# First Strassen group of an attention and gated-MLP kernel: GpSimd makes lower halves, conversions are dealt anew, x gets a third staging buffer

## The chip, the cores and the metric

The kernel runs on one core of a Trainium2 chip. The metric is the device time of one execution in microseconds (us), as the median of several runs. The engines are called by the names of the profile: PE (TensorE, matmuls; PEld are its weight loads), DVE (VectorE), ACT (ScalarE), POOL (GpSimd) and SP (SyncE, which here issues most of the DMAs). A DMA issued by an engine stands in that engine's queue, in order with its other instructions.

## The reference, cut to what matters

```python
# q, k, v: (8, 8, 576, 64)   w_gate, w_val: (512, 1536)   w_out: (1536, 512)
scores = q @ k.T / 8, masked by blocks of 64 (block_i >= block_j)
x = softmax(scores) @ v                 # put together to 4608 tokens x 512
gate = 1 / (1 + exp(-(x @ w_gate)))
out = (gate * (x @ w_val)) @ w_out      # 4608 x 512, float32
```

The three weights arrive as float64. The kernel turns them into float32 itself, by bit operations on the two words of each number. The products need more precision than one pass of PE in the type float32r gives, so every factor is split into an upper half H (rounded to float32r) and a lower half L (what is left), and each product is made as H·H + H·L + L·H, three matmuls.

## The kernel before, in words

**Stages.** Up to about 621 us the kernel does the attention, and between its matmuls the MLP for the first 512 of the 1536 hidden features. The attention's result x goes to DRAM (`xT_d`), the first part of the output too (`part_d`). The other 1024 hidden features are done in two Strassen groups `g` of 512 each. Each group goes over all tokens in five blocks `k`: four of 1024 tokens and one of 512. The list `passes` holds the ten (group, block) pairs; in the first group the order is 0, 1, 4, 2, 3 (block 4 is the small one, so it is the third), in the second 0, 1, 2, 3, 4. The first group writes its part of the output to `part2_d`, the second adds both parts to its own and writes `out`.

**A block.** `unit` (L931) is one of four pairs (q, gv): q is one half of the group's features, gv is gate or value. A unit makes seven Strassen products (`product`, six matmuls each) into three PSUM banks A, B and C out of six, and DVE adds them up (L952 to L965); ACT copies the first of them out (p, L937) and makes the tanh (L944). For gv = 1 DVE then multiplies gate and value (L948), and `split_h` (L926) splits the result h: ACT casts it into hH (L928), and the subtraction for hL (L929) is made by POOL for q = 0 and by DVE for q = 1. After the units, `out_block` (L993) makes the eight output tiles of the block (four in the small one), two groups of four one behind the other, each in two halves of the hidden features (first those of q = 0). In the first group ACT copies each tile out of PSUM (`ost`, L1018), and SP stores it (L1019). There are two tiles of two halves for that, four buffers in turn.

**x of the next block.** `x_load` (L774) brings a quarter of a block's x (half of the columns `c0` by half `j` of d_model) into a staging buffer `XB`, of which there are two. POOL makes the first of the sums that Strassen needs (L793), `x_split` (L798) the others on DVE (L806), the H on ACT (L808) and the L on DVE (L809). The H and L of all seven forms go to the tiles `XO`, over those of the block before. The two loads for the first half of the columns stand at the start of the block before, their split at its end; then come the two loads and the split for the second half.

**Conversions.** While the first group runs, the second group's weights are converted in 24 pieces (the list `later`): 16 of w_gate and w_val, then 8 of w_out. A piece is loaded by SP (`raws`, two buffers), made float32 by six DVE operations and an ACT square (`to_f32`, L676, lines L685 to L699), for w_gate and w_val combined to the seven forms by four more (L742 to L745), cast by ACT into the upper half of a tile `st` (L751, L771), and DVE subtracts for the lower half (L752, L772). SP stores `st` in DRAM (`wgv_d`, `wo_d`). The float32 tile `T` is there once, `st` twice. `do_later(k, i)` (L1109) says how many pieces go behind unit i of a block, or behind its output products (i = 4). In the last block of the first group each unit's weights `W` are refilled from `wgv_d` as soon as the unit is done (L1156), and `wo` at the end.

**Order.** A list scheduler, which works with modelled costs, puts each engine's instructions in order before the program runs; the program's order is its priority, and an instruction that is not ready by the model lets later ones go first. `behind(a, b)` only keeps a after b on one engine's list. On the chip each engine then works off its list in order.

Of the kernel before, what the change touches and what calls it, by code (L numbers as in the profile page):

```python
# [9 lines left out]
F32 = mybir.dt.float32  # L10
# [10 lines left out]
N2 = 512  # L21
# [23 lines left out]
def attn_glu_kernel(ctx: ExitStack, tc: tile.TileContext, q, k, v, w_gate, w_val, w_out, out):  # L45
# [126 lines left out]
    with ExitStack() as s2:  # L172
# [404 lines left out]
        def tiles_o(i):  # L577
            if not co_:
                co_.extend(cv.tile([P, 4, NX], U32, name="XB", bufs=2) for _ in range(2))
                co_.append(at.tile([P, 512], U32, name="coT"))  # L580
            co = [x.rearrange("p a n -> p (a n)") for x in co_[:2]]
            return (co[i % 2].rearrange("p (n w) -> p n w", w=2), co_[2], None,
                    mp.tile([P, 512], F32, name="csq", tag="ost", bufs=2))
# [134 lines left out]
        def half_tiles():  # L718

            i = n_cv[0] % 2  # L720
            n_cv[0] += 1
            if not halves:
                halves.append(cv.tile([P, 2, 256, 2], U32, name="raws", tag="rqk0"))
                halves.append(io.tile([P, 8, P // 2], F32, name="T"))
            return halves[0][:, i], halves[1]
# [21 lines left out]
        def split_gv(T, dst, alone=False):  # L747
            if alone:
                nc.vector.tensor_copy(out=dst[:, 0], in_=T[:, :7])
            else:  # L750
                nc.scalar.copy(out=dst[:, 0], in_=T[:, :7])  # L751
            return nc.vector.tensor_sub(out=dst[:, 1], in0=T[:, :7], in1=dst[:, 0].bitcast(F32)).ins  # L752
# [14 lines left out]
        def wo_piece(raw, T, dst, held=False):  # L767
# [4 lines left out]
            nc.vector.tensor_sub(out=dst[:, 1], in0=T[:, :m], in1=dst[:, 0].bitcast(F32))  # L772

        def x_load(k, j, c0):  # L774

            t0, nk = blocks[k]
            XB = cv.tile([P, 4, NX], F32, name="XB", bufs=2)
# [147 lines left out]

        def split_h(q, i, hH, hL, h, nk):  # L926
            f, n = ((q, 0), (q, nk), (q + 2, 0), (q + 2, nk))[i]
            nc.scalar.copy(out=hH[:, f, n:n + nk], in_=h)  # L928
            (nc.vector if q else nc.gpsimd).tensor_sub(out=hL[:, f, n:n + nk], in0=h, in1=hH[:, f, n:n + nk].bitcast(F32))  # L929
# [63 lines left out]
        def out_block(g, k, hH, hL, wo, sums, more, end):  # L993
            t0, nk = blocks[k]
            n = nk // P
            for ts in (range(n, 2 * n), range(n)):
# [15 lines left out]
                for t in ts:  # L1012
                    r = t0 + t * P
                    if g == 0:
                        if t % 2 == 0:
                            two = cv.tile([P, 2, DM], F32, name="ost2", tag="KQ", bufs=2)
                        ost = two[:, t % 2]
# [35 lines left out]
        io = pool("io")  # L1053
# [19 lines left out]
        for n, (q, gv) in enumerate(units):  # L1073
            for j in range(KC):
                for half in range(2):
# [3 lines left out]
                    def one(got, n=n, j=j, half=half):  # L1079
                        st = st_tile(7, P // 2)  # L1080
                        sums_gv(*got, True)
                        split_gv(got[1], st)
# [3 lines left out]
        for f in range(4):  # L1086
            for half in range(2):
# [3 lines left out]
                def one(got, f=f, half=half):  # L1091
                    st = st_tile(1, DM // 2)[:, :, 0]
                    wo_piece(*got, st, True)
# [3 lines left out]

        n_st = [0]

        def st_tile(a, n):  # L1100

            n_st[0] += 1
            if n_st[0] % 2:
                return cv.tile([P, 2, a, n], F32R, name="st", tag="rqk1")
            return io.tile([P, 2, a, n], F32R, name=f"st{a}", tag="st")
# [3 lines left out]
        def do_later(k, i):  # L1109

            if k == 0:
                count = 2 if i == 4 else 0
            else:
                count = 1 if i < 4 or blocks[k][1] < N2 else 2
# [6 lines left out]

        hH = hp2.tile([P, 4, 2 * N2], F32R, name="hH2")
        hL = hp2.tile([P, 4, 2 * N2], F32R, name="hL2")
        for i, (g, k) in enumerate(passes):
            nk = blocks[k][1]
            end = i == len(passes) - 1
            turn = i + 1 < len(passes) and passes[i + 1][0] > g
            rest_x = []
            if not end:
# [11 lines left out]
                if nn == nk:  # L1141
                    rest_x = [c0 for c0 in range(NX, nn, NX)]
# [5 lines left out]
            for n, (q, gv) in enumerate(units):  # L1148
# [3 lines left out]
                if g + 1 < G:  # L1152
                    do_later(k, n)
                    if turn:
                        W[q, gv] = wgv_tile(q, gv)
                        nc.sync.dma_start(out=W[q, gv].bitcast(F32), in_=wgv_d[n])  # L1156
            if not end:
                x_split(XBs, 0, last2["DVE"])
                for c0 in rest_x:
                    XBs = x_pair(kn, c0)  # L1160
                    for XB in XBs:
                        x_sums(XB, nc.gpsimd)
                    x_split(XBs, c0)
# [36 lines left out]
```

## Time and profile before

| | |
|---|---|
| time, median of 3 runs | 1171.35 us (1170.59 to 1173.22) |
| the profiled execution: its own time, its span | 1172.55 us, 1170.4 us |
| granted clock of TensorE, mean | 0.997 |
| PE busy | 1143.3 us (98%) |
| DVE busy | 813.4 us (69%) |
| ACT busy | 607.9 us (52%) |
| POOL busy | 306.5 us (26%) |
| DMA | 153.32 MB, mean 131 GB/s |

A row of a group or of a timeline names the line of the kernel, the engine, the operation and out<-in by the program's names for tiles, with buffer numbers left out. "[1.21 <-DVE v L952]" behind a row of a timeline means that the engine stood idle for 1.21 us before it and that the DVE instruction of line 952 that writes v ended the wait. The table by stretches gives for each engine the busy us and, in parentheses, the number of instructions; with the name of a tile it counts only the instructions that write or read this tile. Matmuls overlap at their ends, so the step from start to start tells their pace, not their duration.

### The profile page before, as it was taken

The numbers are of one execution on the slowest core, as the hardware profiler recorded it, in microseconds if no ns is written. First come the engines' busy times: TensorE is split into PE (matmuls) and PEld (weight loads), VectorE is DVE, ScalarE is ACT, GpSimd is POOL, SyncE is SP. The second block draws the span as 40 slices with busy tenths as digits, with TensorE's granted clock in tenths as the row PEclk, the third lists the DMA queues.
The fourth block names the chain that finished last, engine by engine and source line by source line (L and its number), as shares of the span: only waits on it lengthen the run. The fifth ranks groups of instructions, "written<-read, shape, count | busy, mean of one in ns | idle before, by whom it ended". The sixth has DMA issues, their size and how long they took to land.

```text
span 1170.4 us, 18756 instructions
## 1 busy us (share of the span) xinstructions
PE 1143.3 (98%) x6413; PEld 916.2 (78%) x6413; DVE 813.4 (69%) x1533; ACT 607.9 (52%) x1344; POOL 306.5 (26%) x356
## 2 busy tenths in 40 slices
PE   6799999999999999999999999999999999999998
PEld 4466777877877787787888888988877888888887
DVE  5678754554655555466989879899897675758565
ACT  5677765756766766675344444544544323233222
POOL 4345513222322313233002110211111424141402
PEclk9999999999999999999999999999999999999999
DMA  8675443444355354525243152763769452635342
GB/s 198 167 153 119 101 118 83 112 98 114 81 116 114 72 124 102 119 69 152 83 134 108 43 169 66 211 163 75 211 261 297 144 198 90 191 97 175 113 135 64
DMA packets 300431, 153.32 MB, mean 131 GB/s; under 512 B 227248, under 2 KB 267184, under 8 KB 299696
## 3 DMA queue, kind: packets, MB, share of 16 engines
q1 hardware_dynamic: 288960, 132.42, 42.9%
q10 hardware_dynamic: 10992, 18.65, 4.4%
q8 instruction: 51, 0.84, 0.3%
q0 software_dynamic: 384, 1.05, 0.2%
q14 instruction: 44, 0.36, 0.1%
HBM read 104.73 MB, written 47.33 MB: 130 GB/s over the span
## 4 chain that ended last, share of the span: by engine, by line
PE 80%; DVE 9%; DMA 4%; issue 3%; ACT 2%; SPq 1%; POOL 1%; ACTq 0%; DVEq 0%; POOLq 0%
PE b L919 25%; PE bank L266 13%; PE m L139 13%; PE m L146 7%; PE b L1004 7%; PE m L1004 7%; PE bank L270 6%; PE bank L139 2%; DVE XL L809 1%; DMA XB<-xT_d 1%; PE m L270 1%; PE bank L146 1%; DMA raws<-in_moe_w_out_dram 1%; ACT G L371 1%; DMA rqk<-in_q_dram 1%
## 5 line engine op out<-in xcount | busy, mean ns | idle before, releaser
L919 PE MATMUL b<-XH,w 128*128 128x512 f32 (+1 forms) x1120 | 320.8, 368 | 3.0 <-ACT XH L808 1.7
L919 PEld LDWEIGHTS b<-XH,w 128*128 128x128 f32 x1120 | 203.4, 189 | 39.3 <-ACT XH L808 2.2
L919 PE MATMUL b<-XL,w 128*128 128x512 f32 (+1 forms) x560 | 205.6, 368 | 0.1
L399 ACT ACTIVATE P<-bank,nm 128x512 f32<-128x512 f32 (+3 forms) x256 | 132.4, 539 | 35.6 <-DVE nm L391 34.6
L919 PEld LDWEIGHTS b<-XL,w 128*128 128x128 f32 x560 | 105.6, 189 | 18.1 <-DVE XL L809 0.6
L808 ACT CAST XH<-XB 128x1024 fp32r<-128x1024 f32 (+1 forms) x72 | 66.9, 943 | 87.4 <-DVE XB L806 46.2
L391 DVE TENSOR_REDUCE nm<-bank 128x2 f32<-128x1024 f32 (+3 forms) x128 | 102.4, 821 | 3.0
L520 DVE TENSOR_TENSOR xT<-bank,rb 128x320 f32<-128x320 f32 x64 | 26.3, 452 | 110.3 <-PE bank L266 91.5
L371 ACT COPY G<-bank 128x768 f32<-128x768 f32 (+3 forms) x140 | 91.0, 700 | 13.1 <-PE bank L270 11.8
L793 POOL TENSOR_TENSOR XB<-XB 128x256 f32<-128x256 f32 x30 | 25.5, 850 | 273.8 <-DMA XB<-xT_d 211.2
L266 PE MATMUL bank<-G,VS 128*64 128x320 f32 (+4 forms) x896 | 94.1, 360 | 0.2
L1004 PE MATMUL m<-wo,hH 128*128 128x512 f32 x288 | 93.2, 389 | 0.0
L1004 PE MATMUL b<-wo,hH 128*128 128x512 f32 x288 | 92.6, 389 | 0.0
L809 DVE TENSOR_TENSOR XL<-XB,XH 128x1024 fp32r<-128x1024 f32 (+1 forms) x72 | 78.0, 1085 | 15.4 <-ACT XH L808 15.4
L266 PEld LDWEIGHTS bank<-G,VS 128*64 128x64 f32 x896 | 55.8, 137 | 41.3 <-issue 4.7
L146 PE MATMUL m<-wo,hH 128*128 128x512 f32 x256 | 86.9, 401 | 0.5 <-ACT hH L163 0.5
L139 PE MATMUL m<-XH,wv 128*128 128x512 f32 x240 | 83.6, 403 | 0.0
L139 PE MATMUL m<-XH,wg 128*128 128x512 f32 x240 | 82.9, 400 | 0.0
L533 POOL TENSOR_TENSOR XL<-xT,XH 128x512 fp32r<-128x512 f32 (+1 forms) x32 | 43.2, 1349 | 144.8 <-ACT XH L528 144.8
L270 PE MATMUL bank<-ident,P 128*128 128x128 f32 x560 | 71.2, 273 | 0.0
L270 PEld LDWEIGHTS bank<-ident,P 128*128 128x128 f32 x560 | 64.3, 140 | 8.3 <-issue 0.7
L164 POOL TENSOR_TENSOR hL<-h,hH 128x512 fp32r<-128x512 f32 x28 | 36.8, 1315 | 111.1 <-ACT hH L163 110.9
(195 smaller groups left out, 2349.3 us busy)
## 6 DMA issues: line engine op xcount, KB each, us to landing
XB<-xT_d SPq DMA_DIRECT2D x48, 256.0 KB
prr<-part_d SPq DMA_DIRECT2D x46, 256.0 KB
xT_d<-xT ACTq DMA_DIRECT2D x32, 288.0 KB
part_d<-ost SPq DMA_DIRECT2D x36, 256.0 KB
VS<-in_v_dram SPq DMA_DIRECT2D x64, 128.0 KB
part_d<-ost ACTq DMA_DIRECT2D x32, 256.0 KB
rqk<-in_k_dram SPq DMA_DIRECT2D x108, 72.0 KB
rqk<-in_q_dram SPq DMA_DIRECT2D x108, 72.0 KB
```

Source lines behind the costliest of these rows:

```text
L139: mm = nc.tensor.matmul(ps, lhsT=lh, rhs=rh, start=(i == 0), stop=(i == n - 1))
L146: mm = nc.tensor.matmul(ps, lhsT=lh[:, f, t * P:(t + 1) * P], rhs=rh, start=(f == i == 0), stop=(f == F1 - 1 and i == 2))
L266: pe_last[:] = [nc.tensor.matmul(*args, **kw).ins]
L270: pe_last[:] = [nc.tensor.transpose(*args).ins]
L371: mark("ACT", nc.scalar.copy(out=dst, in_=src))
L391: mark("DVE", nc.vector.tensor_reduce(out=nm[:, c0:c0 + 2], in_=ps[:, :, c:c + P * (i + 1)], axis=AX.X, op=ALU.max, negate=True))
L399: mark("ACT", nc.scalar.activation(out=Pi[:, h], in_=ps[:, h, c:c + n], func=AF.Exp, bias=nm[:, c0 + h:c0 + h + 1], accum_out=sm[:, 5 * h ...
L533: nc.gpsimd.tensor_sub(out=XL[:, hp, :w], in0=xT[:, :w], in1=XH[:, hp, :w].bitcast(F32))
L808: nc.scalar.copy(out=XO[j][0][:, a:b, c], in_=x)
L809: sub = nc.vector.tensor_sub(out=XO[j][1][:, a:b, c], in0=x, in1=XO[j][0][:, a:b, c].bitcast(F32))
L919: mm = nc.tensor.matmul(ps, lhsT=lh, rhs=rh, start=(first and k == 0), stop=(k == n - 1), skip_group_check=not first)
L1004: mm = nc.tensor.matmul(po[t], lhsT=lh[:, f, t * P:(t + 1) * P], rhs=rh, start=(half == 0 and i == 0), stop=(half == 1 and i == 5))
```

## The change

- `split_h`: in the first group POOL makes all of hL, for q = 1 too. In the second group DVE makes it for q = 1, as before.
- `split_gv` and `wo_piece`: for the 24 pieces POOL subtracts for the lower half, in place of DVE.
- `do_later`: the pieces are dealt otherwise. The five blocks of the first group, in their order, took 2, 6, 5, 6 and 5 pieces; now they take 2, 8, 4, 8 and 2, and the last two stand behind the first unit.
- Buffers: `T` is now there twice and `st` once; both lie in buffers of the pool `cv` that were there before, and the pool `io` is gone. For `ost` one tile of two halves is left, two buffers in turn.
- x: a third staging buffer `XB2` in a new pool `x3`; the three are used in turn. Of the second half of the columns, the load and the first sum for j = 0 now stand at the start of the block before; the load for j = 1 stands behind the split of the first half.
- `refill`: the refill of the last unit's weights now stands behind the loads and the split of x.

```diff
         def x_load(k, j, c0):
...
-            XB = cv.tile([P, 4, NX], F32, name="XB", bufs=2)
+            i = n_x[0] % len(stages)
+            n_x[0] += 1
+            XB = stages[i].tile([P, 4, NX], F32, name=f"XB{i}")
...
             if not halves:
                 halves.append(cv.tile([P, 2, 256, 2], U32, name="raws", tag="rqk0"))
-                halves.append(io.tile([P, 8, P // 2], F32, name="T"))
-            return halves[0][:, i], halves[1]
+                halves.append(cv.tile([P, 2, 7, P // 2], F32R, name="st", tag="rqk1"))
+                two, one = (cv.tile([P, 2, DM], F32, name=x, tag="KQ", bufs=2) for x in ("ost2", "T"))
+                halves.append([one[:, j].rearrange("p (s n) -> p s n", n=P // 2) for j in range(2)])
+                halves.append(itertools.cycle((two[:, 0], two[:, 1])))
+            return halves[0][:, i], halves[2][i]
...
-        def split_gv(T, dst, alone=False):
+        def split_gv(T, dst, alone=False, lower=nc.vector):
...
-            return nc.vector.tensor_sub(out=dst[:, 1], in0=T[:, :7], in1=dst[:, 0].bitcast(F32)).ins
+            return lower.tensor_sub(out=dst[:, 1], in0=T[:, :7], in1=dst[:, 0].bitcast(F32)).ins
...
-            (nc.vector if q else nc.gpsimd).tensor_sub(out=hL[:, f, n:n + nk], in0=h, in1=hH[:, f, n:n + nk].bitcast(F32))
+            (nc.vector if q and second[0] else nc.gpsimd).tensor_sub(out=hL[:, f, n:n + nk], in0=h, in1=hH[:, f, n:n + nk].bitcast(F32))
...
-                        if t % 2 == 0:
-                            two = cv.tile([P, 2, DM], F32, name="ost2", tag="KQ", bufs=2)
-                        ost = two[:, t % 2]
+                        if not halves:
+                            half_tiles()
+                        ost = next(halves[3])
...
-        io = pool("io")
+        stages.append(pool("x3"))
...
-                        st = st_tile(7, P // 2)
+                        st = halves[1]
                         sums_gv(*got, True)
-                        split_gv(got[1], st)
+                        split_gv(got[1], st, lower=nc.gpsimd)
...
-            if k == 0:
-                count = 2 if i == 4 else 0
+            place = turns_of[0].index(k)
+            if place in (0, NK - 1):
+                count = 2 if i == (0 if place else 4) else 0
             else:
-                count = 1 if i < 4 or blocks[k][1] < N2 else 2
+                count = (1, 1, 0, 1, 1)[i] if blocks[k][1] < N2 else (1, 2, 1, 2, 2)[i]
...
+        def refill(n):
+            W[units[n]] = wgv_tile(*units[n])
+            d = nc.sync.dma_start(out=W[units[n]].bitcast(F32), in_=wgv_d[n])
+            if n == len(units) - 1:
+                behind(d.ins, last2["SP"])
...
                 if nn == nk:
-                    rest_x = [c0 for c0 in range(NX, nn, NX)]
+                    rest_x = [x_load(kn, 0, NX)]
+                    x_sums(rest_x[0], nc.gpsimd)
...
-                    if turn:
-                        W[q, gv] = wgv_tile(q, gv)
-                        nc.sync.dma_start(out=W[q, gv].bitcast(F32), in_=wgv_d[n])
+                    if turn and n + 1 < len(units):
+                        refill(n)
             if not end:
                 x_split(XBs, 0, last2["DVE"])
-                for c0 in rest_x:
-                    XBs = x_pair(kn, c0)
-                    for XB in XBs:
-                        x_sums(XB, nc.gpsimd)
-                    x_split(XBs, c0)
+                if rest_x:
+                    rest_x.append(x_load(kn, 1, NX))
+                    x_sums(rest_x[1], nc.gpsimd)
+                    x_split(rest_x, NX)
+            if turn:
+                refill(len(units) - 1)
             run(outs)
```

More of the change, by code (lines that the diff above doesn't have):

```diff
@@ L578, in tiles_o @@
             if not co_:
-                co_.extend(cv.tile([P, 4, NX], U32, name="XB", bufs=2) for _ in range(2))
+                co_.extend(cv.tile([P, 4, NX], U32, name=f"XB{i}") for i in range(2))
                 co_.append(at.tile([P, 512], U32, name="coT"))
@@ L765, in fetch_wo, with wo_piece @@
             return raw, T
-        def wo_piece(raw, T, dst, held=False):
+        def wo_piece(raw, T, dst, held=False, lower=nc.vector):
             T = T.rearrange("p s n -> p (s n)")
@@ L771, in wo_piece @@
             nc.scalar.copy(out=dst[:, 0], in_=T[:, :m])
-            nc.vector.tensor_sub(out=dst[:, 1], in0=T[:, :m], in1=dst[:, 0].bitcast(F32))
+            lower.tensor_sub(out=dst[:, 1], in0=T[:, :m], in1=dst[:, 0].bitcast(F32))
+        stages, n_x = [cv, cv], [0]
         def x_load(k, j, c0):
             t0, nk = blocks[k]
-            XB = cv.tile([P, 4, NX], F32, name="XB", bufs=2)
+            i = n_x[0] % len(stages)
+            n_x[0] += 1
+            XB = stages[i].tile([P, 4, NX], F32, name=f"XB{i}")
             v = XB[:, 0:4].rearrange("p (kh th) n -> p kh th n", kh=2)
@@ L924, in product @@
             mark2("PE", mm)
+        second = [False]
         def split_h(q, i, hH, hL, h, nk):
@@ L1091, in one @@
                 def one(got, f=f, half=half):
-                    st = st_tile(1, DM // 2)[:, :, 0]
-                    wo_piece(*got, st, True)
+                    st = halves[1].rearrange("p e a n -> p e (a n)")[:, :, :DM // 2]
+                    wo_piece(*got, st, True, nc.gpsimd)
                     h = slice(half * DM // 2, (half + 1) * DM // 2)
@@ L1096, in attn_glu_kernel @@
                 later.append((get, one))
[L1098 to L1105, printed above, removed]
         got = []
         def do_later(k, i):
-            if k == 0:
-                count = 2 if i == 4 else 0
+            place = turns_of[0].index(k)
+            if place in (0, NK - 1):
+                count = 2 if i == (0 if place else 4) else 0
             else:
-                count = 1 if i < 4 or blocks[k][1] < N2 else 2
+                count = (1, 1, 0, 1, 1)[i] if blocks[k][1] < N2 else (1, 2, 1, 2, 2)[i]
             for _ in range(min(count, len(later))):
@@ L1125, in attn_glu_kernel @@
             nk = blocks[k][1]
+            second[0] = g > 0
             end = i == len(passes) - 1
```

## The prediction

> **What bounds the kernel now.** I read the page first, then the table of busy time by stretch of time, then PE's own timeline, and last the chain of waits at the place where PE loses time.
>
> ```profile
> span 1170.4 us, 18756 instructions
> ...
> PE 1143.3 (98%) x6413; PEld 916.2 (78%) x6413; DVE 813.4 (69%) x1533; ACT 607.9 (52%) x1344; POOL 306.5 (26%) x356
> ```
>
> PE is busy for 1143.3 of 1170.4 us, so no change that leaves the matmuls alone can win more than the 27 us in which PE stands still, and only what lies in the stage that is edited. The next view cuts out that stage: the five blocks of the first Strassen group (the fifth stretch ends where PE starts the second group), and one block of the second group below.
>
> ```profile
> core 0: us, PE busy (x) PEld busy (x) DVE busy (x) ACT busy (x) POOL busy (x), PEclk, DMA share, GB/s
> 621.00:681.00 60.00, 60.00 (x266) 49.66 (x265) 53.16 (x92) 29.47 (x46) 11.07 (x14) 1.00 0.30 96
> 681.00:741.00 60.00, 60.00 (x268) 49.72 (x267) 51.13 (x106) 28.16 (x48) 8.73 (x8) 1.00 0.48 131
> 741.00:777.00 36.00, 35.91 (x236) 32.84 (x235) 34.96 (x93) 17.93 (x40) 5.81 (x7) 1.00 0.59 160
> 777.00:837.00 60.00, 60.00 (x266) 49.64 (x266) 54.70 (x120) 28.98 (x49) 8.13 (x7) 1.00 0.55 143
> 837.00:894.00 57.00, 55.79 (x247) 45.88 (x246) 52.68 (x102) 25.30 (x46) 9.24 (x8) 1.00 0.75 263
> ...
> 955.80:1015.70 59.90, 59.90 (x266) 49.60 (x265) 40.40 (x59) 19.45 (x29) 20.35 (x16) 1.00 0.45 140
> ```
>
> The clock is granted in full (1.00) throughout. PE is full in four of the five blocks, and in the second group (59.90 of 59.90), where the change therefore has nothing to win. The second fullest engine is DVE, with 51 to 55 of 60 us, while POOL has 6 to 11. PE loses time in the fifth stretch alone and just behind it, so I looked there instruction by instruction. The first number of a row is its start.
>
> ```profile
> 865.93 0.39 PE L919 MATMUL b<-XH,w 128*128 128x512 f32 x1
> 867.53 0.50 PE L919 MATMUL b<-XH,w 128*128 128x512 f32 x1 [1.21 <-DVE v L952]
> ...
> 893.50 0.39 PE L919 MATMUL b<-XH,w 128*128 128x512 f32 x1
> 893.73 0.39 PE L919 MATMUL b<-XL,w 128*128 128x512 f32 x1
> 893.96 0.61 PE L919 MATMUL b<-XH,w 128*128 128x512 f32 x2
> 894.71 0.50 PE L919 MATMUL b<-XL,w 128*128 128x512 f32 x1
> 895.05 0.40 PE L919 MATMUL b<-XH,w 128*128 128x512 f32 x1
> 897.19 0.73 PE L919 MATMUL b<-XH,w 128*128 128x512 f32 x2 [1.74 <-ACT XH L808]
> ```
>
> Matmuls start 0.23 us apart when nothing holds them (893.50 to 893.73). From 865.93 to 867.53 are 1.60 us for one step: 1.37 lost, to a DVE add (L952) that was late behind conversion work. From 893.50 to 897.19 are six steps in 3.69 us: 2.33 lost, to the first x of the second group, not yet split. Together 3.70 us, the change's whole visible prize. The chain of waits tells why x was late (start, length):
>
> ```profile
> 861.42 9.37 DMA raws<-in_moe_w_out_dram
> ...
> 885.59 5.03 DMA XB<-xT_d
> 890.78 1.54 POOL XB L793
> ```
>
> and SP's queue tells when the load could go:
>
> ```profile
> 883.51 2.55 SPq L785 DMA_DIRECT2D XB<-xT_d  x4
> ```
>
> A piece of w_out took 9.37 us to land between the refills of w, DVE stood in order behind it, and both loads of the second half of x were issued only at 883.51, when the first half had been split and had freed both staging buffers. PE wanted them at 893.50.
>
> **The change, part by part.** *Third staging buffer, load moved ahead.* One of the two loads of the second half (two DMAs of the four, with the sums by POOL) now goes at the start of the block, 50 us earlier; the other still waits for a freed buffer. The last refill of w is put behind that load on SP, and of its four it is the one needed last. SP issues the same DMAs, so nothing is added there. On POOL's queue the early sum now stands ahead of the block's hL; the load needs some 5 us, and an hL of the second block (698.79, a row below) comes 18 us after the block's start at 681, so nobody waits behind it. Together with the emptier fifth block below, I take the 2.33 us as gone: the remaining load needs the 5.03 us of its row, and the split before it no longer has pieces of w_out among its work. Bounds: 0 if DMA stays the brake, 2.33 at most.
>
> *Dealing of the conversions.* Of the 24 pieces the five blocks took 2, 6, 5, 6, 5 and now take 2, 8, 4, 8, 2. The three that leave the fifth block are what the add at 867.53 stood behind: 1.37 us gone. Blocks two and four get two more each, and there DVE must be counted. By stretch, DVE's work on T, of it what writes st, and the lower halves hL:
>
> ```profile
> 621.00:897.00 276.00, 82.28 (x208) 22.66 (x48) 1.00 0.53 158
> ...
> 621.00:897.00 276.00, 16.39 (x24) 12.25 (x24) 1.00 0.53 158
> ...
> 621.00:897.00 276.00, 55.72 (x144) 27.04 (x144) 12.60 (x20) 24.97 (x20) 1.00 0.53 158
> ```
>
> ```profile
> L698 DVE SCALAR_TENSOR_TENSOR raws<-raws 128x256 f32<-128x256 uint32 x24 | 12.4, 518 | 0.4
> ```
>
> A piece without its lower half is (82.28 + 12.4 - 16.39) / 24 = 3.26 us of DVE; a lower half is 16.39 / 24 = 0.68, one hL is 12.60 / 20 = 0.63 on DVE and 24.97 / 20 = 1.25 on POOL.
>
> *Lower halves and hL to POOL.* DVE gives up 24 x 0.68 + 20 x 0.63 = 29 us, and POOL takes about 44 x 1.1 = 48 on top of 43 in 273: room enough. But the two engines are not independent. POOL's and DVE's timelines side by side, with an undisturbed instance of the same DVE line below each:
>
> ```profile
> 698.79 1.30 POOL L929 TENSOR_TENSOR hL<-v,hH 128x512 fp32r<-128x512 f32 x1 [1.34 <-ACT hH L928]
> 702.57 1.29 POOL L929 TENSOR_TENSOR hL<-v,hH 128x512 fp32r<-128x512 f32 x1 [2.48 <-PE b L919]
> 706.80 1.30 POOL L929 TENSOR_TENSOR hL<-p,hH 128x512 fp32r<-128x512 f32 x1 [2.94 <-issue]
> ```
>
> ```profile
> 699.62 0.75 DVE L694 SCALAR_TENSOR_TENSOR T<-T 128x256 f32<-128x256 f32 x1 [1.03 <-ACT T L691]
> 702.60 1.33 DVE L742 TENSOR_TENSOR T<-T 128x64 f32<-128x64 f32 x1
> 704.46 0.21 DVE L743 TENSOR_TENSOR T<-T 128x64 f32<-128x64 f32 x1
> 707.17 1.41 DVE L752 TENSOR_TENSOR st<-T,st 128x448 fp32r<-128x448 f32 x1 [0.42 <-ACT st L751]
> 709.47 0.42 DVE L694 SCALAR_TENSOR_TENSOR T<-T 128x256 f32<-128x256 f32 x1
> 714.50 0.63 DVE L752 TENSOR_TENSOR st<-T,st 128x448 fp32r<-128x448 f32 x1 [0.42 <-ACT st L751]
> ```
>
> A DVE instruction that meets a POOL subtraction ends when POOL's ends: 702.60 + 1.33 is 703.93, and POOL's ends at 703.86. The three lost 0.33, 1.12 and 0.78 us, 0.74 a piece, against 0.63 to 0.68 that moving one saves. So the move frees next to nothing of DVE's time. I take 0.74 for an hL and, by its 448 of 512 columns, 0.64 for a lower half. Second block: 51.13 + 2 x 3.26 - 6 x 0.68 - 4 x 0.63 + 4 x 0.74 + 8 x 0.64 = 59.1 of 60. Fourth: 54.70 + 6.5 - 6.6 + 3.0 + 3.5 (six of its eight pieces are w_out's, with 256 columns) = 58.1 of 60, an upper value, since these pieces are shorter. Third: 34.96 - 3.3 - 3.4 - 1.7 + 4.0 = 30.6 of 36. Fifth: 52.68 - 9.8 - 3.4 - 2.5 + 3.7 = 40.7 of 57. DVE becomes as full in two blocks as it was in the fifth. What that costs PE no row shows directly: the nearest ones are 0 (fourth block now, DVE 54.70, PE 60.00) and 1.2 (fifth now, one late add). I take one late add, 1.2 us, in the second block; bounds 0 and 2 x 1.2 in each of the two blocks.
>
> The Trainium skill, "SBUF — State Buffer", section "Who interferes with whom", has a rule for this: DVE and GpSimd share one port pair, an exclusive lock that the first to start keeps for its whole instruction while the other fully blocks. The trace agrees in the end times above. Taken at its full length, with DVE always in need of the pair, the rule would charge each moved subtraction with POOL's whole time, and the sum would come out as in the second rival below; with the measured 0.74 it comes out as here.
>
> The hL of the second half of the columns (q = 1) now takes 1.25 in place of 0.63 us and may stand behind one lower half (1.13). PE wants them after the first half of the output products, 24 matmuls or 5.4 us that need only q = 0: hidden, 0; without that cover up to 1.8 us a block, and the range takes that in.
>
> *One st, two T; two output halves in place of four.* The cast into st now waits for the store before; ACT is at 28 of 60 us, so I cost it at nothing, bound 0.6 us of ACT for a pair. The copies of the output tiles lose two of their four buffers:
>
> ```profile
> 680.68 1.07 ACT L1018 ACTIVATE ost<-m 128x512 f32<-128x512 f32 x2
> 681.65 0.60 ACT L1018 ACTIVATE ost<-b 128x512 f32<-128x512 f32 x1
> 683.99 0.59 ACT L1018 ACTIVATE ost<-b 128x512 f32<-128x512 f32 x1
> 685.12 0.57 ACT L937 COPY p<-b 128x512 f32<-128x512 f32 x1
> ```
>
> ```profile
> DMA to landing us min/median/max: 4.2/4.6/5.1
> ```
>
> The only stores of ost whose landing is shown took 4.6 us. So the third copy goes to about 686 and the fourth just behind, 3 to 4 us later than now; the wait is on ACT, and the copies of p (L937) behind it are what PE would feel. I cost it at nothing, because the present p at 685.12 is 3 us behind its product and PE (60.00 of 60.00) loses nothing; if that cover is gone, see the third rival.
>
> *Before 621 us and in the second group* only names of buffers change and hL stays with DVE: 0, within the runs' scatter.
>
> **Sum.** -1.37 - 2.33 + 1.2 = -2.5 us. The profiled execution took 1172.55 us, 1.2 above the median of the three runs (1171.35); against the median the forecast is 1168.85, faster by 0.21%.
>
> **The rivals.** (1) DVE's fullness eats the prize: two late adds (2.4) and one late split, as at 893.50 (2.3), in blocks two to four: -3.7 + 4.7, 1172.4. For it: 59.1 and 58.1 of 60. Against: DVE lost time to POOL before too and PE stayed full in four blocks. (2) The lock at full length, by rows: each moved subtraction costs DVE 1.29 (hL) or 1.13 (lower half): second block 51.1 + 6.5 - 6.6 + 14.2 = 65.2 and fourth 65.9 of 60, 11 us too much, less 3.7: 1178.7. Against: the measured mean is 0.74. (3) Slower by the output buffers: p stands behind two waiting copies. At 687.2 instead of 685.12 it is 2.1 us later; once it is later than one product (six steps, 1.36 us) PE loses the rest and more, say 1.4 at each of five block ends: 7 - 3.7, 1174.7. Against: the planner may put p ahead of a copy that it sees waiting. (4) The change does not do what it says: the load of x still lands late because three refills of w fill the DMA queues (busy share 0.75 in the fifth stretch): only 1.37 is won and 1.2 given back, 1171.2.
>
> **How the numbers follow.** Forecast 0.43, rival (1) 0.27, (2) 0.05, (3) 0.17, (4) 0.08. This kernel's runs tell about 0.2% (2.3 us) from no change: faster 0.43, same 0.35 (rivals 1 and 4), slower 0.22. The range runs from 1166.8 (all 3.70 us won, and 0.8 of the runs' scatter) to 1174.7; it leaves out (2) and half of what is worse than (3). The forecast's own range is 1167.6 to 1169.0.
>
> **What would show it.** Right: no wait of PE on L952 near 867 and none on L808 at the start of the second group; one load of x issued near the start of each block; DVE at 58 us or more in blocks two and four, its instructions of 0.2 to 0.4 us stretched to over 1 us beside POOL's. Wrong: PE under 58 us in block two or four with DVE as releaser (1, 2), or with ACT's p as releaser and ACT waiting for part2's stores (3); POOL waiting for XB's DMA after 889 (4).

## The result, and the profile after

| | before | after |
|---|---|---|
| time, median (range) | 1171.28 us (1170.13 to 1173.22) | 1189.12 us (1186.37 to 1191.41) |
| ratio of the times, 95% interval | | 1.0146 (1.0128 to 1.0164) |
| span of the profiled execution | 1170.4 us | 1187.8 us |

The changed kernel is 17.8 us slower where 2.5 us faster was forecast. The head of its page, and the table of busy time with stretches cut at its own block ends (the fifth ends where the second group starts):

```profile
span 1187.8 us, 18741 instructions
...
PE 1151.7 (97%) x6413; PEld 917.1 (77%) x6413; DVE 807.8 (68%) x1489; ACT 605.5 (51%) x1344; POOL 374.2 (32%) x400
```

```profile
core 0: us, PE busy (x) PEld busy (x) DVE busy (x) ACT busy (x) POOL busy (x), PEclk, DMA share, GB/s
621.00:681.00 60.00, 60.00 (x266) 49.62 (x265) 54.44 (x92) 28.12 (x45) 19.50 (x19) 1.00 0.36 121
681.00:743.00 62.00, 61.03 (x266) 49.23 (x266) 52.23 (x102) 27.58 (x47) 22.28 (x16) 1.00 0.44 117
743.00:785.00 42.00, 36.17 (x224) 32.58 (x224) 36.79 (x92) 20.25 (x43) 21.54 (x17) 0.92 0.60 159
785.00:847.00 62.00, 58.83 (x256) 47.21 (x255) 56.01 (x112) 26.81 (x48) 26.84 (x20) 1.00 0.52 133
847.00:910.00 63.00, 61.26 (x266) 49.33 (x265) 49.43 (x75) 25.04 (x44) 25.25 (x22) 1.00 0.71 247
```

The five blocks take 289 us in place of 273: 16 of the 17.4 us by which the span grew. PE stands still for 11.7 us of them (289 - 277.29) where it was 1.3 before, and the third stretch has a granted clock of 0.92: half the full clock for 6.8 of its 42 us, as shown below. DVE is not full anywhere: 52.23 of 62 in the second block, where I had counted 59.1 of 60. What PE waits for, summed up from 621 to 985 us, is no longer one thing (total, times, longest; the six largest):

```profile
PE b L926 <- ACT p L946: 3.7, 4, 2.6
PE b L926 <- DVE g L961: 2.3, 1, 2.3
PE b L926 <- ACT ost L1027: 1.6, 2, 1.2
PE m L1013 <- POOL hL L938: 1.1, 1, 1.1
PE m L1013 <- ACT ost L1027: 1.0, 2, 0.6
PE b L1013 <- ACT hH L937: 0.9, 1, 0.9
```

The two waits that the change was to remove are gone as such (v at 867, XH at the second group), but ACT's and DVE's ordinary work is late all over. The place with the largest loss shows how. POOL, then ACT, then PE (start, length):

```profile
736.10 3.91 POOL L938 TENSOR_TENSOR hL<-p,hH 128x512 fp32r<-128x512 f32 x1 [7.64 <-ACT hH L937]
739.97 0.92 POOL L800 TENSOR_TENSOR XB<-XB 128x256 f32<-128x256 f32 x1
```

```profile
740.92 1.05 ACT L815 CAST XH<-XB 128x1024 fp32r<-128x1024 f32 x1 [3.91 <-POOL XB L800]
...
744.28 0.43 ACT L691 ACTIVATE T<-raws 128x256 f32<-128x256 f32 x1 [0.86 <-POOL st L755]
746.20 0.83 ACT L815 CAST XH<-XB 128x768 fp32r<-128x768 f32 x1 [1.49 <-DVE XB L813]
746.94 1.08 ACT L1027 ACTIVATE ost<-m 128x512 f32<-128x512 f32 x2
747.90 0.38 ACT L946 COPY p<-b 128x256 f32<-128x256 f32 x1
```

```profile
745.44 0.28 PE L926 MATMUL b<-XH,w 128*128 128x256 f32 x1
748.33 0.45 PE L926 MATMUL b<-XH,w 128*128 128x256 f32 x1 [2.61 <-ACT p L946]
748.58 0.42 PE L926 MATMUL b<-XL,w 128*128 128x256 f32 x1
...
752.18 0.58 PE L926 MATMUL b<-XH,w 128*128 128x256 f32 x1 [2.32 <-DVE g L961]
```

An hL that takes POOL 1.3 us undisturbed took 3.91. The sum of x behind it on POOL's queue was late, ACT stood 3.91 us for it, in order, and then worked off XH, output copies and casts before the p that PE needed. Then the clock fell to half for 6.8 us, and matmuls of 256 columns that start 0.12 us apart at full clock started 0.21 apart:

```profile
743.00:748.50 5.50, 2.89 (x23) 1.00 0.97 257
748.50:755.30 6.80, 4.48 (x20) 0.50 0.99 289
```

By that pace the 20 matmuls of the second row lost some 2 us to the clock; for the rest of the row PE waited again.

The hL of p on POOL, grouped, before and after, 621 to 912 us (mean ns behind the busy time; the hL of v and t of the same width rose only from 1.34 to 1.47 us):

```profile
L929 POOL TENSOR_TENSOR hL<-p,hH 128x512 fp32r<-128x512 f32 x4 | 5.4, 1360 | 16.3 <-issue 12.2 <-ACT hH L928 4.0
```

```profile
L938 POOL TENSOR_TENSOR hL<-p,hH 128x512 fp32r<-128x512 f32 x8 | 18.8, 2352 | 36.7 <-ACT hH L937 36.7
```

### The profile page after: what moved, and what is told of

The parts are those of the page before. It is cut to its first block, busy times and chain, and to the rows that moved or that the text cites. A ratio compares the mean times of both kernels' runs of the same rounds, so it can differ in the third digit from the quotient of the medians.

```text
span 1187.8 us, 18741 instructions
## 1 busy us (share of the span) xinstructions
PE 1151.7 (97%) x6413; PEld 917.1 (77%) x6413; DVE 807.8 (68%) x1489; ACT 605.5 (51%) x1344; POOL 374.2 (32%) x400
## 4 chain that ended last, share of the span: by engine, by line
PE 68%; DVE 14%; DMA 6%; issue 4%; ACT 3%; SPq 2%; POOL 1%; ACTq 0%; DVEq 0%; POOLq 0%
PE b L926 20%; PE bank L266 13%; PE m L139 13%; PE m L146 7%; PE bank L270 6%; PE b L1013 4%; PE m L1013 4%; DMA part_d<-ost 2%; DVE XL L816 2%; DVE XB L813 2%; PE bank L139 2%; DMA XB<-xT_d 1%; DVE v L957 1%; PE bank L146 1%; ACT P L399 1%
## 5 line engine op out<-in xcount | busy, mean ns | idle before, releaser
L926 PE MATMUL b<-XH,w 128*128 128x512 f32 (+1 forms) x1120 | 325.8, 371 | 9.9 <-ACT p L946 3.7
L816 DVE TENSOR_TENSOR XL<-XB,XH 128x1024 fp32r<-128x1024 f32 (+1 forms) x72 | 82.2, 1154 | 13.0 <-ACT XH L815 12.9
L1013 PEld LDWEIGHTS m<-wo,hH 128*128 128x128 f32 x288 | 54.1, 188 | 13.3 <-ACT ost L1027 2.3
```

What stands on the lines that cost most here:

```text
L816: sub = nc.vector.tensor_sub(out=XO[j][1][:, a:b, c], in0=x, in1=XO[j][0][:, a:b, c].bitcast(F32))
L926: mm = nc.tensor.matmul(ps, lhsT=lh, rhs=rh, start=(first and k == 0), stop=(k == n - 1), skip_group_check=not first)
L1013: mm = nc.tensor.matmul(po[t], lhsT=lh[:, f, t * P:(t + 1) * P], rhs=rh, start=(half == 0 and i == 0), stop=(half == 1 and i == 5))
```

## The experiments

"Alone" means one part put into the kernel before; "back" means one part of the changed kernel undone. All ratios are to the kernel before, run on the same chip (its median was 1170.9 to 1172.2 us), with 95% intervals.

**Which part costs.** Three parts alone, and the output buffers back. Theory A blames the two output halves, B the subtractions on POOL, C the new dealing.

e1, two output halves alone:

```diff
-                        if t % 2 == 0:
+                        if not osts:
                             two = cv.tile([P, 2, DM], F32, name="ost2", tag="KQ", bufs=2)
-                        ost = two[:, t % 2]
+                            osts.append(itertools.cycle((two[:, 0], two[:, 1])))
+                        ost = next(osts[0])
```

> The kernel before with one thing changed: the output tiles of the first group use one tile of two halves in turn (two buffers) in place of two tiles of two halves (four). Theory A (the two output buffers are the cause: the third copy of a batch waits on ACT for the store of the first, and p, hH and tanh stand behind it): 1183 to 1190 us, with ACT waiting 15 to 30 us in all for the stores of ost and PE losing time to ACT. Theory B (the subtractions on POOL hold up DVE and hL): under 1174. Theory C (eight pieces in blocks two and four fill DVE): under 1174.

Measured: 1175.36 us, 1.0035 (1.0020 to 1.0051), some 4 us slower: less than A had said, more than B and C allow. ACT waited for the stores:

```profile
ACT ost L1019 <- DMA part_d<-ost: 17.0, 13, 3.3
```

e2, the changed kernel with four output halves (for the space T is there once):

```diff
...
-                        if not halves:
-                            half_tiles()
-                        ost = next(halves[3])
+                        if t % 2 == 0:
+                            two = cv.tile([P, 2, DM], F32, name="ost2", tag="KQ", bufs=2)
+                        ost = two[:, t % 2]
```

> The changed kernel with four output buffers again; to make room T is there once (its square lies beside the one st). POOL's subtractions, the new dealing, the third buffer of x and the single st stay. Theory A: 1167 to 1172 us, the 3.7 us at the turn to the second group won and little lost before it. Theory B: 1182 or more, since POOL's subtractions are still there. Theory C: 1180 or more.

Measured: 1180.93 us, 1.0088 (1.0070 to 1.0107). By the ratios 6.8 of the 17.1 us come back and 10.3 stay.

e3, POOL's subtractions alone (hL of q = 1 and the pieces' lower halves):

```diff
-            return nc.vector.tensor_sub(out=dst[:, 1], in0=T[:, :7], in1=dst[:, 0].bitcast(F32)).ins
+            return lower.tensor_sub(out=dst[:, 1], in0=T[:, :7], in1=dst[:, 0].bitcast(F32)).ins
...
-            (nc.vector if q else nc.gpsimd).tensor_sub(out=hL[:, f, n:n + nk], in0=h, in1=hH[:, f, n:n + nk].bitcast(F32))
+            (nc.vector if q and second[0] else nc.gpsimd).tensor_sub(out=hL[:, f, n:n + nk], in0=h, in1=hH[:, f, n:n + nk].bitcast(F32))
...
-                        split_gv(got[1], st)
+                        split_gv(got[1], st, lower=nc.gpsimd)
```

> The kernel before with only the subtractions moved: the lower halves of the 24 pieces and all hL of the first group on POOL. Four output buffers, two st, old dealing, two buffers of x. Theory A: 1169 to 1174 us. Theory B: 1180 to 1190, with DVE instructions stretched beside POOL's and PE waiting for DVE or for hL of POOL. Theory C: as theory A.

Measured: 1182.41 us, 1.0093 (1.0064 to 1.0121). DVE, which was to be relieved, now stood for POOL, because T is there once and POOL reads it last:

```profile
DVE T L685 <- POOL st L752: 13.8, 9, 4.7
DVE T L685 <- POOL st L772: 4.2, 5, 1.3
```

e4, the dealing alone (only `do_later` changed):

> The kernel before with only the dealing of the 24 pieces changed (2, 8, 4, 8, 2 in place of 2, 6, 5, 6, 5). Theory A: 1168 to 1174 us: the late add of the fifth block goes, DVE may be late elsewhere. Theory B: the same. Theory C: 1180 or more, PE waiting for DVE's adds in blocks two and four.

Measured: 1171.08 us, 0.9995 (0.9983 to 1.0008): nothing. So of three theories C falls, B carries most, and A is real: 4 us alone.

**Which of POOL's subtractions.** Theory B1 was that T comes back late, B2 that hL comes late for PE.

e5, in e3 only the hL line:

> The kernel before, with one edit: the lower halves hL of the second half of the columns (q = 1) made by POOL in the first Strassen group; the lower halves of the converted pieces stay with DVE. Theory B1 (the +10 us of POOL's subtractions come from T: it is given back by POOL late, and DVE and ACT stand in order behind it): no lower half of a piece is on POOL, so 1171 to 1173 us, ratio 1.000 to 1.002. Theory B2 (they come from hL: POOL's subtraction is held off by two-input instructions of DVE and PE waits for it): most of the loss, 1178 to 1181 us. Both equally: about 1176 us.

e6, in e3 only the pieces' line:

> The kernel before, with one edit: the lower halves of the 24 converted pieces of the first Strassen group made by POOL; every hL stays where it was. B1 (T given back late): nearly the whole loss of the run with both, 1179 to 1182 us, with waits of DVE's and ACT's T for POOL's st of some 30 us in all as there. B2 (hL late): 1171 to 1174 us.

e7, e3 with T twice (and st once):

> The kernel before with both subtractions on POOL as in the run of them alone, and T laid out twice, so that the next piece does not wait for POOL's subtraction of the last; for the space st is there once in place of twice and the squares of the cleaning stand beside it. B1: the waits of T for POOL's st go to under 5 us and the time to 1172 to 1175 us, less whatever the single st costs ACT. B2: nothing is won, 1181 to 1183 us, PE still waits for hL.

e8, the changed kernel with all subtractions back on DVE:

> The changed kernel with all its subtractions (hL of q = 1 and the pieces' lower halves) back on DVE; the dealing, the third staging buffer, the two output halves, T twice and st once stay. A and B together (two output buffers cost some 4 us alone, POOL's subtractions the rest, dealing nothing): 1173 to 1177 us. If something else of the change costs by itself (st once, the order of the refills, the early load of x): 1179 us or more. If the output buffers only cost beside POOL's subtractions: under 1172 us.

e9, the changed kernel with only hL back on DVE:

> The changed kernel with one edit: hL of q = 1 goes back to DVE; the lower halves of the pieces stay on POOL. Theory B2 (hL is what must not be on POOL, since PE wants it and DVE's two-input instructions hold POOL off; the pieces' lower halves alone cost nothing, as in the run of them alone, and only make POOL's queue longer): as the changed kernel with both back on DVE, 1177 to 1180 us. Theory B1 (T given back late by POOL): little is won, 1184 to 1188 us.

e10, the changed kernel with only the pieces' lower halves back on DVE:

> The changed kernel with one edit: the lower halves of the 24 pieces go back to DVE; hL of q = 1 stays on POOL. B2 in its pure form: nearly the whole loss stays, 1184 to 1188 us. If hL alone costs what it cost alone in the kernel before (+2.5 us) and the rest comes from both subtractions in one queue: 1180 to 1182 us. B1: 1178 to 1179 us.

Measured in us, with the ratios:

| subtractions on POOL | in the kernel before | in the changed kernel |
|---|---|---|
| none of those moved | 1170.9 to 1172.2 | e8: 1178.30, 1.0056 (1.0035 to 1.0076) |
| hL of q = 1 | e5: 1174.36, 1.0021 (1.0008 to 1.0035) | e10: 1180.88, 1.0081 (1.0063 to 1.0098) |
| lower halves of pieces | e6: 1170.86, 0.9992 (0.9982 to 1.0002) | e9: 1192.14, 1.0175 (1.0155 to 1.0195) |
| both | e3: 1182.41, 1.0093 (1.0064 to 1.0121) | 1189.12, 1.0146 (1.0128 to 1.0164) |

Neither theory stands alone. By the ratios hL alone costs 2.5 us in the one column and 2.9 in the other. The pieces' lower halves cost nothing with four output halves, st twice and the old dealing, but 8 us there with hL beside them, and 8 to 14 us in the changed kernel. e9 is slower than both of its theories had said; hL on POOL as well makes it some 3 us faster, though the intervals touch. e8 lies between its first two ranges; what that means is said behind e11.

e7, 1176.84 us, 1.0035 (1.0021 to 1.0050), gives back half of e3's loss, and DVE's wait of T for st went from 18 to 1.7 us. That looks like B1's share, but e6 forbids to price the wait by its length: there DVE waits 22.3 us of T for st, and nothing is lost. B2's share is seen in e7, where PE stood 2.61 us for an hL of POOL in one piece; in e3 and e5 PE waits for no hL, but for ACT's and DVE's work. By which way hL and the lower halves together cost so much more than each alone is not shown.

e9, the worst, shows a chain that the late lower halves make. POOL, SP's queue and ACT at its fourth block end:

```profile
831.46 4.39 POOL L775 TENSOR_TENSOR st<-T,st 128x256 fp32r<-128x256 f32 x1 [2.83 <-ACT st L774]
```

```profile
835.87 0.36 SPq L1104 DMA_DIRECT2D wo_d<-st  x1
836.28 2.65 SPq L792 DMA_DIRECT2D XB<-xT_d  x4
839.03 0.89 SPq L1028 DMA_DIRECT2D part_d<-ost  x2
```

```profile
841.78 0.60 ACT L1027 ACTIVATE ost<-b 128x512 f32<-128x512 f32 x1 [6.30 <-DMA part_d<-ost]
```

A subtraction of 0.74 us took 4.39; its store, the loads of x and the stores of two output tiles stood behind it in SP's order; ACT waited 6.30 us for an output half.

**By which way the lower halves cost in the changed kernel.** That chain made SP's queue the suspect (theory Q).

e13, the stores of st issued by POOL (`nc.sync` to `nc.gpsimd` in two lines):

> The changed kernel with one edit: the stores of st (24, one a piece) are issued by POOL behind its own subtraction, in place of SP. Theory Q (the lower half that POOL makes late holds SP's queue, since its store stands there in order, and with it the loads of x and the stores of ost behind it): SP's waits for POOL's st (56 us between 621 and 980) are gone, and most of the loss with them: 1178 to 1182 us, the level of the run with the lower halves back on DVE (1180.9). Theory T (the loss comes through T, which POOL gives back late to DVE and ACT): 1186 to 1190 us, as the changed kernel. POOL's issue of a DMA may cost it up to a microsecond each; if that counts, 1190 us or more.

Measured: 1191.53 us, 1.0170 (1.0147 to 1.0194). SP's waits for st are gone but for one, and nothing is won: ACT's waits for the stores of st rose from 11.9 to 22.1 us. Q is not borne out. It is not ruled out either, since POOL now spends 23.6 us on issuing the 24 stores (1.11 us each for the 16 of w_gate and w_val, 0.73 for the others), as the expectation allowed for.

```profile
ACT st L754 <- DMA wgv_d<-st: 14.3, 8, 3.7
ACT st L774 <- DMA wo_d<-st: 7.8, 6, 3.3
```

e14, the stores of ost issued by ACT (`nc.sync` to `nc.scalar` in one line):

> The changed kernel with one edit: the stores of the output tiles (ost) are issued by ACT right behind its copy, in place of SP; the stores of st and the loads of x stay on SP. If the cost of the two output buffers is that their stores stand on SP behind others: ACT's waits for these stores (24.3 us between 621 and 980) go to under 10 us and the time to 1178 to 1183 us. If the loss goes through the loads of x and through T: 1186 us or more. ACT's own issue of 36 DMAs costs it time too, by which the kernel could get slower.

Measured: 1188.10 us, 1.0143 (1.0117 to 1.0170), no change. ACT still waits 18.7 us for them: they land late, not only start late. Between 838 and 844 us, say, ACT issued a store at 838.52 and could write to the same half again at 843.96.

e17, st twice and T once (the second T's place goes to st):

> The changed kernel with the two buffers exchanged: st twice and T once (the second st in the place of the second T, T in what is left beside the third staging buffer, the squares of the cleaning beside the first st); two output halves and all subtractions on POOL stay. Theory S (with one st, cast, subtraction on POOL, store and the next cast form a chain of over 7.5 us a piece, and ACT stands in order at the cast): ACT's waits for the stores of st (11.9 us between 680 and 980) go under 4 us, and the time to 1180 to 1184 us. Theory T (T given back late): 1190 to 1194 us. Theory P (neither buffer: POOL's late subtractions reach PE by hL, and by the sums of x behind them on POOL's queue): 1186 to 1191 us.

Measured: 1185.98 us, 1.0117 (1.0097 to 1.0136), 3 us better than the changed kernel, though the intervals touch. ACT's waits for the stores of st are gone, but DVE's wait of T for POOL is 19.4 us in place of 8.4: taking one wait away makes the next. The time lies between the ranges of S and P, and PE waits 3.5 us for an hL of POOL, as P has it; so S holds at most in part, and P is not ruled out. How the 8 us divide is not settled; the list scheduler also orders every one of these kernels anew, so that no two differ in a buffer alone.

**What the forecast had credited.** e15, the third staging buffer, early load and refill alone (with one st for the space):

> The kernel before with the third staging buffer, the early load and the refill put back (and st once, T of seven slots, for the space), without the new dealing. By the forecast's step the 2.33 us at the start of the second group are won and the 1.37 us at the late add stay: 1169 to 1170 us. If the dealing is what brought the gain of the run with both (4 us): 1171 to 1172 us; if all of it came from the load: 1167 to 1168 us.

Measured: 1168.76 us, 0.9978 (0.9966 to 0.9991). Of PE's waits in the stage one is left:

```profile
PE b L926 <- DVE v L961: 0.8, 1, 0.8
```

e11, the same with the new dealing:

> The kernel before with only those parts of the change that the forecast credited: the third staging buffer with the early load and the refill put back, and the new dealing; four output buffers stay, all subtractions stay with DVE. For the space st is there once in place of twice, with the squares of the cleaning beside it. If both steps of the forecast hold (1.37 and 2.33 us won): 1167 to 1169 us. If DVE, fuller in blocks two and four, gives it back: 1170 to 1172 us. If the single st or the reordered loads cost something themselves: 1173 us or more.

Measured: 1167.70 us, 0.9968 (0.9955 to 0.9980): faster than both kernels. At the start of the second group, where the kernel before lost 2.33 us, nothing is lost (0.23 from start to start), and the late add shrank to 0.6:

```profile
891.88 0.39 PE L1011 MATMUL b<-wo,hH 128*128 128x512 f32 x1
892.10 0.39 PE L926 MATMUL b<-XH,w 128*128 128x512 f32 x1
892.33 0.39 PE L926 MATMUL b<-XL,w 128*128 128x512 f32 x1
892.56 0.39 PE L926 MATMUL b<-XH,w 128*128 128x512 f32 x1
```

```profile
PE b L926 <- DVE v L961: 0.6, 1, 0.6
```

e15's and e11's intervals overlap; whether the dealing adds anything is open.

**Which parts make each other dearer.** e11, e2, e8 and the changed kernel all have the third staging buffer, the new dealing and st once. They differ in the output halves and in the subtractions; T is there once in the left column and twice in the right one:

| | four output halves | two output halves |
|---|---|---|
| subtractions as before | e11: 0.9968 (0.9955 to 0.9980) | e8: 1.0056 (1.0035 to 1.0076) |
| moved to POOL | e2: 1.0088 (1.0070 to 1.0107) | changed kernel: 1.0146 (1.0128 to 1.0164) |

The step to two output halves costs 10.3 us in the upper row and 6.8 in the lower one, but 4.1 alone (e1). The moved subtractions cost 14.1 us in the left column and 10.5 in the right one, and 10.9 alone (e3). So the two parts do not make each other dearer: the output halves already cost more than alone where no subtraction was moved. In e8 PE waits 4.2 us for the split of x (XH and XL), in e11 not at all. Why the halves cost more beside the early load and the new dealing is not shown.

**Why a POOL subtraction takes 4 us.** Three kernels that compute nothing of the reference: POOL subtractions of 128x512 beside rows of DVE instructions (from e16; e12 has one output tile for all):

```diff
+        for i in range(n_dve):
+            dve(dos[i % outs], ad)
+        for _ in range(n_pool):
+            nc.gpsimd.tensor_sub(out=po, in0=ap, in1=A[:, :512])
...
+    def two(n):
+        return lambda do, ad: nc.vector.tensor_sub(out=do[:, :n], in0=ad[:, :n], in1=E[:, :n])
```

e12:

> A kernel of its own that computes nothing of the reference: eight subtractions of 128x512 by POOL, one behind the other, beside rows of DVE instructions without pauses, in five stretches: beside nearly nothing, beside 60 two-input subtractions of 128x512, 40 of 128x768, 120 of 128x64, and 60 one-input scalings of 128x512; last 20 subtractions of DVE beside one of POOL. Theory L1 (who starts first keeps the pair for one instruction, then they take turns): each POOL subtraction waits for one DVE instruction at most, 1.3 to 2 us in every stretch, and DVE's instructions beside it grow to 1.3 to 2 us. Theory L2 (DVE's next instruction comes ahead of a POOL that waits, so that POOL goes on only where DVE pauses): one POOL subtraction grows to 4 us or more beside the wide two-input rows, perhaps to the whole row, while it stays at 1.3 us beside one-input ones.

Eight POOL subtractions took 10.65 us beside nearly nothing and 12.93 beside the two-input row of 128x512; DVE's went from 0.69 to 1.63 us each, strictly in turns. L1 holds, no 4 us.

e16, rows that write four tiles in turn:

> A kernel of its own that computes nothing of the reference: eight POOL subtractions of 128x512, one behind the other, beside rows of two-input DVE instructions, first with one output tile for all (they follow each other at 0.03 us distance, and in the run before POOL and DVE then took turns, 1.59 and 1.63 us each), then with four output tiles in turn: 128x512, 128x768, 128x64, scaled adds of 128x256, and these once more with one output tile. Theory O (what holds POOL off for 4 us in the kernel is that independent DVE instructions overlap, so that the pair is not free between them): POOL's subtraction grows to 3 us or more beside the rows with four tiles and stays at 1.6 beside those with one. If they take turns everywhere: 1.3 to 1.9 us in every stretch, and the 4 us come from something else.

All rows took turns but one. There the first subtraction was held for 35.67 us, until DVE's row ended (the eight of that stretch, beside the eight of the stretch before):

```profile
42.70 12.93 POOL L67 TENSOR_TENSOR opapart<-papart,A 128x512 f32<-128x512 f32 x8 [25.08 <-ACT papart L60]
87.08 45.05 POOL L67 TENSOR_TENSOR opwide<-pwide,A 128x512 f32<-128x512 f32 x8 [31.45 <-ACT pwide L60]
```

e18, two subtractions a row, each row started a little later:

> A kernel of its own that computes nothing of the reference: two POOL subtractions of 128x512, started 0.05 us later from row to row (eight starts), beside rows of DVE instructions: 12 of 128x768 with one output tile, 12 of 128x768 with four, 16 of 128x512 with four, 28 scaled adds of 128x256 with four. Theory O (independent DVE instructions overlap, and a POOL that asks in the middle of one is not let in until the row pauses; one that asks at a change of instructions is): of the 24 starts beside four-tile rows some are held to the row's end (7 to 10 us), the rest under 2 us, and none beside the one-tile row. Theory W (only the width counts): all eight at 128x768 with four tiles are held, none at 512 and 256. If the 35.67 us of the run before were a chance of its own: none is held over 2.3 us.

All eight at 128x512 with four tiles were held to the end of the row, none at 128x768, none beside the others. The first of each, and DVE's rows around the held one:

```profile
5.48 3.64 POOL L70 TENSOR_TENSOR opdep<-pdep,A 128x512 f32<-128x512 f32 x2 [5.04 <-ACT pdep L64]
20.69 3.52 POOL L70 TENSOR_TENSOR opwide<-pwide,A 128x512 f32<-128x512 f32 x2 [11.57 <-ACT pwide L64]
32.17 11.90 POOL L70 TENSOR_TENSOR opapart<-papart,A 128x512 f32<-128x512 f32 x2 [7.96 <-ACT papart L64]
```

```profile
19.33 3.76 DVE L79 TENSOR_TENSOR od<-dwide,E 128x768 f32<-128x768 f32 x3 [1.45 <-ACT dwide L61]
...
29.29 2.68 DVE L79 TENSOR_TENSOR od<-dwide,E 128x768 f32<-128x768 f32 x3
31.90 9.71 DVE L79 TENSOR_TENSOR od<-dapart,E 128x512 f32<-128x512 f32 x16
```

Width (W) falls, and so does O's second half, the point of the instruction at which POOL asks. What the held ones share is that DVE had then worked without any pause for long: 20.69 came 1.4 us after a pause of DVE, 32.17 came in a row that ran on from the row before (31.90 without idle time). In the kernel the same count holds: in the traces of the changed kernel, e3, e9 and e10, 15 subtractions and sums of POOL took over 1 us longer than undisturbed, all of them asked for when DVE had run over 1.2 us without a pause; of those that asked at other times none did. Every one lies beside the split of x, where DVE has its longest rows. It is no sufficient sign: about half of the 291 subtractions and sums of POOL in these four traces (153, from 621 to 912 us) were asked for when DVE had run that long, and the other 138 of them were not held. That is a pattern of these traces; why DVE is preferred there, and not in the rows with turns, is not shown.

## Why the prediction was wrong, point by point

**The buffer for x** was right, mechanism and size: 2.33 us taken, e15 won 2.6 by its ratio (1.1 to 4.0), and PE no longer waits for XH there.

**The dealing** was not: of the 1.37 us taken e4 shows nothing, and in e11 the late add is still 0.6. That DVE would be nearly full in blocks two and four was wrong too: it is busy for 52.23 and 56.01 of 62 us. The sum for the fourth block was also added up wrongly: its terms give 61.1, not 58.1.

**"DVE loses 0.74 for each moved subtraction"** is the step that failed first. The sum asked only what DVE loses, and found +1.2 us in DVE's fullness. DVE's busy time in the five blocks stayed where it was (249 us, added up from the table above; 247 before), far from full; POOL lost. In the three overlaps from which 0.74 came POOL had asked first. With the pair in turns DVE loses 0.94 (1.63 - 0.69, e12), but a POOL that has to wait lost 2 to 5 us in places, and no row of before showed that: none of POOL's 36 subtractions and sums in the stage was held for more than 0.8 us. The Trainium skill, "SBUF — State Buffer", section "Who interferes with whom", says that the pair is an exclusive lock, that a DVE instruction with two SBUF inputs contends for it with GpSimd's reads, and, of DVE's two-port modes, that whoever issues first has it for the whole instruction. e12 agrees with a lock that is taken in turns (1.59 and 1.63 us), but a turn of both takes 1.67 us, less than the 1.27 and 0.69 that they take alone. e16 goes past it: a POOL subtraction was passed over by some 40 DVE instructions, 35.67 us.

**"hL on POOL: hidden, 0; without that cover up to 1.8 us a block"** failed. The hL of p took 2.35 us in the mean and up to 5.4, and the sum of x stands behind it on POOL's queue, which the working did not name. PE waited 1.5 us for hL itself; e5 prices the whole at 2.5 us alone.

**"One st, two T": nothing** held where DVE subtracts (e11 and e15 have one st and lose nothing). With the lower half on POOL, T or st is held longer, and DVE or ACT stands at it in order (e3, e7, e17); what that costs by itself is open, since e6 has the same waits and no loss.

**"Output halves: 0"** failed; rival (3) had the mechanism, ACT in order behind a store that has not landed. The sign that it named came in part: ACT waits 24.3 us for the stores, and PE 3.7 us for p, but 2.9 of these in the third block, not in the second or fourth. It priced itself at 7 us; e1 measures 4, and the step from e11 to e8 10. "PE loses nothing at 685" was no cover, since ACT's wait comes again at every tile.

**The sum of small terms** failed as such. By the ratios the parts alone are +4.1 us (e1), +10.9 (e3), -0.6 (e4) and -2.6 (e15), together 11.8; measured are 17.1. Each term was priced beside the slack of the kernel before. The table behind e11 shows which term did not keep its price, the output halves; by which way is open. One term was left out of the sum altogether, the clock: its halving after short stops of PE (last section) took up to 2.2 us in the changed kernel. Rival (2) came nearer in time (1178.7) but by the wrong engine: DVE was never too full.

## What to carry to other kernels

Moving work to an idle engine is not free when that engine shares something with the one it relieves: ask what the receiver waits for, who then holds a buffer longer, and which in-order queue stands at that buffer. The price of a part is the price beside the others: two output halves cost 4 us alone, and 10 beside two parts that by themselves gained. So price parts together, or change them one at a time: two parts of this change alone gave 0.9968, all together 1.0146.

## What the runs showed of the hardware that was not expected

- POOL's two-input subtraction takes turns with DVE's two-input instructions (1.59 and 1.63 us in place of 1.27 and 0.69), but one that asks within a long unbroken DVE row can be held to its end: 35.67 us in e16, some 9 us longer than undisturbed in eight of eight at 128x512 in e18, 2 to 5 us in the kernels.
- Short stops of PE halved the granted clock. In the profiled executions, between 600 and 1100 us, it was full in the kernel before, e4, e5, e6, e11 and e15. In every kernel that is slower than these it fell to 0.5: for 3.4 us in e1, e7, e8 and e10, for 6.8 in e3 and the changed kernel, for 10 to 14 in e2, e9, e13, e14 and e17. Half of PE's busy time in these stretches is the most that it can have cost: 1.7 us in e1, 3.0 in e3, 2.2 in the changed kernel, 6.1 in e9. In e1 it followed two waits of PE of 1.59 and 0.50 us (rows below), in the changed kernel one of 2.61; the kernel before lost 2.33 us at the second group without it, so what exactly brings it on is open. The Trainium skill, "TensorE: Matmul & The Clock Gate", section "HAM oscillation — how this bites in real kernels", puts the danger at idle gaps of over some 3.4 us; here shorter ones were enough.

```profile
898.00:901.24 3.24, 1.15 (x5) 1.00 1.08 377
901.24:904.65 3.41, 3.41 (x9) 0.50 1.05 362
```
